# Retention attention in halves of 64 tokens with a state in the middle, and weight decoding inside the raw weight tile

## The chip, the cores and the metric

The kernel runs on one core of a Trainium2 chip. The metric is the device time of one execution in microseconds (us), median of several runs. The core has five engines that run side by side and wait for each other on semaphores: TensorE (PE in the profile; PEld is its loading of weights), VectorE (DVE), ScalarE (ACT), GpSimd (POOL) and SyncE (SP), which issues the DMAs here.

## The reference

A retention (linear attention with decay) over 4 sequences of 768 tokens with 8 heads of 64, and behind it a feed-forward layer on all 3072 tokens whose activation is a ratio of two polynomials:

```python
for t in range(S):                                   # S = 768, D = 64, 8 heads, 4 sequences
    state = gamma * state + einsum('bhd,bhe->bhde', k[:, :, t], v[:, :, t])
    y[:, :, t] = scale * einsum('bhd,bhde->bhe', q[:, :, t], state)
x = y.transpose(0, 2, 1, 3).reshape(3072, 512)
h = x @ w_in                                         # 512 -> 2048
g = (a0 + a1*h + a2*h*h + a3*h**3) / (1 + abs(b0)*abs(h) + abs(b1)*h*h + 1e-6)
out = g @ w_out                                      # 2048 -> 512
```

## The kernel before, in words

**Chunks and slots.** The attention is done in 24 chunks of 128 tokens, six to a sequence (`C = 6`, the chunk's place in its sequence is `c`). Four chunks make a block of 512 tokens, six blocks in all. The feed-forward layer runs in 96 slots: a slot `(n, f)` takes block `n` and 128 of the 2048 inner units. A slot has `gemm_in` (12 matmuls 128x512 into a PSUM tile `ph`, of which there are two), the polynomials on ACT, DVE and POOL (`poly_scalar`, `poly_vector`, `ratio_scalar`, `ratio_vector`, `split`), and `gemm_out` (12 matmuls into four `po` tiles), which runs three slots later (`LAG = 3`). Full precision comes from splitting each operand into a high and a low part (`xh`/`xl`, `gh`/`gl`, two parts of each weight), hence 12 matmuls where four would do.

**Order.** All five queues are in the order in which the code is written. `opening()` does the four chunks of block 0 and decodes the first weight tiles; then `run()` goes over the slots. The chunks of block `n` lie in the slots ahead of it, in two parts each: part 0 (scores and mask) behind a slot's `gemm_out`, part 1 (the rest) between a later slot's `gemm_in` and `gemm_out`. Blocks 1 and 2 have a part in every slot (slots 0 to 7 and 24 to 31), blocks 3 to 5 in every second slot from 32 to 78. Slots 8 to 23 and 80 to 95 hold no attention.

**One chunk.** `scores` (L249) multiplies keys and queries, in quarters of the PE array (64 rows by 64 columns, `64*64` in the profile): late keys with late queries, and early keys with all queries, so half of its matmuls have 128 columns to stream and half have 64. The two other results go to the banks `pa`. `mask` (L266) multiplies them on DVE with a causal table into `aT`. `recall` (L290) multiplies the state from before the chunk with all 128 queries, in quarters of 128 columns. `outer` (L276) forms keys times values over all 128 tokens, in halves of the array (`128*64`). `values` (L320) multiplies `aT` with the values: the later half over 128 rows (`128*64`), the earlier over 64 (`64*64`). Quarters that write into one bank at once are kept apart by a semaphore that SP passes on (`gate`, L315). `update` (L338) adds the new outer product to the single tile `state`; `scale_state` on POOL lets it decay. `x_out` splits the result into `xh` (ACT) and `xl` (DVE). Each of these f32 matmuls is two records in the profile, two passes over the same columns: 8 matmuls are `x16` there.

**Weights.** A weight tile arrives as 64-bit floats, two 32-bit words `raw[:, :, 0]` (low) and `raw[:, :, 1]` (high), one DMA of 512 KB, 32 tiles in all. ACT reads some bits of the low word into `t` (`decode_low`, L132) and the high word into `u` (`decode_high`, L140). DVE joins them in two instructions (`decode_join`, L148 and L151, called the two joins below). ACT rounds to the high part (`decode_split`, L164), POOL takes the difference (`decode_rest`, L171). A tile is decoded in each of the slots 3 to 24. `u` lies in PSUM:

```python
    def u_bank():
        if not opened:                       # in opening(): the two ph banks
            return early_bank("u", f"ph{count['u'] % 2}", U32)
        ...
        return bank("u", U32)                # later: the two banks that pa and px use in turn
```

`bank` (L61) hands the two banks `bank0` and `bank1` out in turn, to `pa`, to `px` and to `u`; whoever comes next waits until the last owner is done.

**Loads.** Each chunk needs `kT`, `qT`, `v` and `k`, 256 KB each, double-buffered. In the opening SP issues them in this order, chunk by chunk, with weight tiles between; in `run()` `kT` of chunk `i + 2` comes in part 0 of chunk `i`, the other three in part 1. POOL scales `qT` and `v` (L227, L233).

Of the kernel before, what the change touches and what calls it, by code (L numbers as in the profile page):

```python
# [16 lines left out]
P = 128  # L17
# [4 lines left out]
def tile_retention_rational_ffn(  # L22
# [35 lines left out]
    count = {"ph": 0, "bank": 0, "u": 0}  # L58
    opened = []

    def bank(name, dtype=F32):  # L61
        tag = "ph" if name == "ph" else "bank"
        count[tag] += 1
        return ps.tile([P, TB], dtype, name=name, tag=f"{tag}{count[tag] % 2}")
# [5 lines left out]
    def u_bank():  # L70

        if not opened:
            count["u"] += 1
            return early_bank("u", f"ph{count['u'] % 2}", U32)
        if len(opened) < 2:
            count["u"] += 1
            return early_bank("u", f"po{count['u'] % 2}", U32)
        if len(opened) < 3:
            return early_bank("u", f"po{SPB - 1}", U32)
        return bank("u", U32)  # L80

    def px_banks(i):
        if len(opened) < 2:
            return [early_bank("px", f"po{r + 2 * (i % 2 or i >= SPB)}") for r in range(2)]
        return [bank("px") for _ in range(2)]


    causal_sb = const.tile([P, 3, HP], F32, name="causal_sb")
# [7 lines left out]
    state = const.tile([P, NP, D], F32, name="state")  # L96
# [37 lines left out]
    def decode_high(i):  # L134
        if i >= len(tiles):
            return


        us[i] = u_bank()
        nc.scalar.activation(  # L140
            us[i].bitcast(F32), raws[i][:, :, 1].bitcast(F32), AF.Abs, scale=2.0 ** -112
        )
# [58 lines left out]
    def load_k_t(i):  # L201
        load_part(i, "kT", kT, 0, [P, NP, P])

    def load_rest(i):
        load_part(i, "qT", qT, 1, [P, NP, P])
        load_part(i, "v", v, 3, [P, H, D])
        if i % C < C - 1:
            load_part(i, "k", kk, 2, [P, H, D])
# [10 lines left out]

    def quarters(r, j):  # L220
        odd = (r + j) % 2
        lo, hi = slice(odd * HP, (odd + 1) * HP), slice((1 - odd) * HP, (2 - odd) * HP)
        return lo, hi, slice(0, 2 + odd, 1 + odd), 1 + odd
# [12 lines left out]

    def scale_state(i):
        if i < NSTEP and i % C > 0:
            nc.gpsimd.tensor_mul(
                state, state, sdec_sb.unsqueeze(2).broadcast_to([P, NP, D])  # L240
            )

    def pa_banks(i):
        st = steps[i]
        if "banks" not in st:
            st["banks"] = [bank("pa") for _ in range(2)]
        return st["banks"]

    def scores(i):  # L249
        st = steps[i]  # L250
        pa = [x[:, : 3 * P].rearrange("p (a b t) -> p a b t", a=2, b=3) for x in pa_banks(i)]
        for late in range(2):
            for a in range(2):
                for j in range(2):
                    for r in range(2):
                        rows = slice(r * D, (r + 1) * D)
                        lo, hi, both, own = quarters(r, j)
                        nc.tensor.matmul(  # L258
                            pa[r][hi, a, own] if late else pa[r][lo, a, both],
                            st["kT"][rows, 2 * a + j, late * HP : (late + 1) * HP],  # L260
                            st["qT"][rows, 2 * a + j, late * HP :],
                            start=True, stop=True,
                        )
        st["pa"] = pa

    def mask(i):  # L266
        st = steps[i]
        for r in range(2):
            st["aT", r] = at.tile([P, 2, 3, HP], F32, name="aT")
            nc.vector.tensor_mul(  # L270
                st["aT", r], st["pa"][r],
                causal_sb.unsqueeze(1).broadcast_to([P, 2, 3, HP]),
            )


    def outer(i, first):  # L276
        st = steps[i]
        if first or i % C == 0:
            st["px"] = px_banks(i)
        if i % C < C - 1:  # L280
            pk = st["pk"] = st["px"][1][:, TB // 2 :].rearrange("p (h d) -> p h d", d=D)
            for aj in range(NP):
                for r in range(2):
                    h = 4 * (aj // 2) + 2 * r + aj % 2
                    nc.tensor.matmul(  # L285
                        pk[r * D : (r + 1) * D, aj], st["k"][:, h], st["v"][:, h],
                        start=(first or i % C == 0), stop=True, skip_group_check=True,
                    )

    def recall(i, first):  # L290
        st = steps[i]
        if i % C > 0:
            if first:
                st["px"] = px_banks(i)

            for a in range(2):
                for j in range(2):
                    for r in range(2):
                        rows = slice(r * D, (r + 1) * D)
                        st["recalled"] = nc.tensor.matmul(  # L300
                            st["px"][r][j * D : (j + 1) * D, a * P : (a + 1) * P],
                            state[rows, 2 * a + j], st["qT"][rows, 2 * a + j],
                            start=(a == 0), stop=False, skip_group_check=True,
                        )
# [10 lines left out]
    def gate(i):  # L315
        if i % C > 0:
            steps[i]["gate"] = nc.sync.nop()
            after(steps[i]["gate"], steps[i]["recalled"])

    def values(i, lates=(1, 0)):  # L320
        st, c = steps[i], i % C
        for late in lates:
            for a in range(2):
                for j in range(2):
                    for r in range(2):
                        lo, _, _, own = quarters(r, j)
                        s, b = (slice(0, P), own) if late else (lo, 0)
                        t = a * P + late * HP
                        x = nc.tensor.matmul(  # L329
                            st["px"][r][j * D : (j + 1) * D, t : t + HP],  # L330
                            st["v"][s, 4 * a + 2 * r + j], st["aT", r][s, a, b],
                            start=(c == 0 and late == 1 and a == 0),
                            stop=(c == 0 or a == 1), skip_group_check=True,
                        )
                        if late == 0 and c > 0 and (a, j, r) == (0, 0, 0):
                            after(x, st["gate"])

    def update(i):  # L338
        if i % C < C - 1:
            if i % C == 0:  # L340
                return nc.vector.tensor_copy(state, steps[i]["pk"])
            return nc.vector.tensor_add(state, steps[i]["pk"], state)

    def x_parts(i, r):
# [20 lines left out]
    def opening():  # L365
# [14 lines left out]
        for i in range(SPB):  # L380
# [4 lines left out]
            if i + 1 < SPB:  # L385
                fill(i + 1, FILL[1])
# [325 lines left out]
```

## Time and profile before

| | us |
|---|---|
| median of three runs (637.66, 639.0, 639.3) | 639.0 |
| the profiled execution: from its first to its last instruction | 636.5 |
| PE busy | 614.6 |
| ACT busy | 440.4 |
| DVE busy | 437.3 |
| POOL busy | 362.7 |

What an execution takes around its instructions isn't in the trace; the median is 2.5 us over the profiled execution's span. A row of a group reads: line, engine, operation, output <- inputs, sizes, count, then busy time of the group and mean duration of one instruction, then how long the engine stood idle ahead of such instructions and who ended that. In the chain of work that ended last, and in the timeline, a row is: start, duration (us), engine, what. Neighbouring matmuls overlap, so distances between starts say more of PE than durations do.

### The profile page before, as it was taken

To read this page: it belongs to the slowest core of one execution; us is meant where nothing else is said; L and a number is where in the kernel's file an instruction comes from. 1 tells how busy PE (TensorE), PEld (TensorE's weight loads), DVE (VectorE), ACT (ScalarE), POOL (GpSimd) and SP (SyncE) were. 2 spreads that over 40 slices of the span, in tenths; PEclk is the share of its full clock that TensorE was granted. 3 is DMA by queue.
4 is the path that set the end of the run, shared out by engine and by line. 5 is a ranking of instruction groups with operands and counts; after the bars stand their busy time and mean duration, and the time that the engine had idled before them with its cause. 6 is when DMAs were issued, how large, how long until landed. Compare 5 with 4: busy or idle time off the path is not lost.

```text
span 636.5 us, 11515 instructions
## 1 busy us (share of the span) xinstructions
PE 614.6 (97%) x4508; PEld 495.8 (78%) x4508; DVE 437.3 (69%) x684; ACT 440.4 (69%) x721; POOL 362.7 (57%) x311
## 2 busy tenths in 40 slices
PE   7598999999999999999999999999999999999997
PEld 4386778888877878788888878888878888888885
DVE  3668888888887666766666676666666656766663
ACT  2678889889886557566657676675766576777773
POOL 3858678888866554563644554544456443444442
PEclk9888999999999999999999999999999999999999
DMA  9976672001016222310110321121301000100001
GB/s 319 399 262 233 220 274 90 1 1 66 1 52 198 67 68 83 132 50 19 50 50 18 117 67 34 35 51 34 112 22 34 2 0 2 57 10 1 1 1 66
DMA packets 24389, 52.48 MB, mean 82 GB/s; under 512 B 3088, under 2 KB 3216, under 8 KB 24336
## 3 DMA queue, kind: packets, MB, share of 16 engines
q1 hardware_dynamic: 24336, 51.76, 23.8%
q8 instruction: 35, 0.57, 0.4%
q14 instruction: 18, 0.15, 0.1%
HBM read 43.36 MB, written 8.39 MB: 81 GB/s over the span
## 4 chain that ended last, share of the span: by engine, by line
PE 70%; ACT 10%; DVE 9%; issue 4%; DMA 1%; POOL 0%; POOLq 0%; SPq 0%; DVEq 0%; ACTq 0%
PE ph L424 32%; PE po L479 30%; PE px L329 3%; ACT ph L453 2%; ACT s L452 2%; DVE q L456 2%; DVE ph L457 2%; ACT t L132 2%; DVE p L458 2%; PE pa L258 2%; PE px L300 1%; PE px L285 1%; DMA v<-in_v 1%; DVE p L447 1%; ACT s L441 1%
## 5 line engine op out<-in xcount | busy, mean ns | idle before, releaser
L442 POOL TENSOR_TENSOR q<-q,s 128x512 f32<-128x512 f32 x96 | 124.6, 1298 | 216.9 <-ACT s L441 209.8
L424 PE MATMUL ph<-xh,w 128*128 128x512 f32 (+2 forms) x776 | 211.4, 395 | 5.2 <-DVE t L151 3.4
L479 PE MATMUL po<-w,gh 128*128 128x512 f32 x768 | 200.2, 393 | 0.0
L424 PEld LDWEIGHTS ph<-xh,w 128*128 128x128 f32 x776 | 145.3, 191 | 36.3 <-ACT u L140 3.6
L479 PEld LDWEIGHTS po<-w,gh 128*128 128x128 f32 x768 | 142.7, 188 | 30.5 <-POOL w L171 0.2
L435 ACT ACTIVATE q<-ph 128x512 f32<-128x512 f32 x96 | 57.2, 596 | 116.1 <-PE ph L424 115.9
L447 DVE TENSOR_TENSOR p<-ph,p 128x512 f32<-128x512 f32 x96 | 66.1, 689 | 95.1 <-ACT p L443 95.0
L464 POOL TENSOR_TENSOR gl<-p,gh 128x512 fp32r<-128x512 f32 x96 | 124.7, 1299 | 7.3 <-issue 4.5
L479 PE MATMUL po<-w,gl 128*128 128x512 f32 x384 | 110.6, 390 | 0.2 <-POOL gl L464 0.2
L424 PE MATMUL ph<-xl,w 128*128 128x512 f32 (+2 forms) x388 | 104.7, 392 | 0.0
L456 DVE SCALAR_TENSOR_TENSOR q<-q,qcon,ph 128x512 f32<-128x512 f32 x96 | 71.4, 743 | 48.4 <-ACT ph L453 48.1
L424 PEld LDWEIGHTS ph<-xl,w 128*128 128x128 f32 x388 | 74.0, 192 | 15.5
L452 ACT ACTIVATE s<-q,qcon 128x512 f32<-128x512 f32 x96 | 69.4, 723 | 22.9 <-POOL q L442 22.9
L479 PEld LDWEIGHTS po<-w,gl 128*128 128x128 f32 x384 | 72.1, 188 | 15.6 <-POOL gl L464 0.6
L448 DVE SCALAR_TENSOR_TENSOR p<-p,par_sb,ph 128x512 f32<-128x512 f32 x96 | 71.8, 748 | 3.4
L443 ACT ACTIVATE p<-ph,par_sb 128x512 f32<-128x512 f32 x96 | 73.3, 764 | 0.0
L457 DVE SCALAR_TENSOR_TENSOR ph<-p,par_sb,ph 128x512 f32<-128x512 f32 x96 | 71.9, 749 | 0.0
L458 DVE SCALAR_TENSOR_TENSOR p<-q,ph 128x512 f32<-128x512 f32 x96 | 65.9, 686 | 3.3
L463 ACT CAST gh<-p 128x512 fp32r<-128x512 f32 x96 | 58.7, 612 | 13.5 <-DVE p L458 13.5
L441 ACT ACTIVATE s<-q,babs 128x512 f32<-128x512 f32 x80 | 65.4, 817 | 2.7
L453 ACT ACTIVATE ph<-s 128x512 f32<-128x512 f32 x96 | 57.8, 602 | 11.5 <-DVE p L448 2.2
L171 POOL TENSOR_TENSOR w<-t,w 128x512 fp32r<-128x512 f32 x32 | 41.3, 1294 | 0.8 <-ACT w L164 0.8
(38 smaller groups left out, 426.6 us busy)
## 6 DMA issues: line engine op xcount, KB each, us to landing
raw<-in_w_in SPq DMA_DIRECT2D x16, 512.0 KB, 5.5
raw<-in_w_out SPq DMA_DIRECT2D x16, 512.0 KB, 6.8
kT<-in_kT SPq DMA_DIRECT2D x24, 256.0 KB, 2.8
qT<-in_qT SPq DMA_DIRECT2D x24, 256.0 KB, 3.2
v<-in_v SPq DMA_DIRECT2D x24, 256.0 KB, 3.2
out<-o SPq DMA_DIRECT2D x24, 256.0 KB, 2.3
k<-in_k SPq DMA_DIRECT2D x20, 256.0 KB, 3.5
half<-o SPq DMA_DIRECT2D x8, 256.0 KB, 2.2
```

The costliest lines, as they stand in the source:

```text
L424: nc.tensor.matmul(ph[:, t0:t1], w1[f][:, part, kt * P : (kt + 1) * P], x[:, kt, t0:t1], start=(i == 0), stop=(i == 3 * NP - 1),)
L441: nc.scalar.activation(s, q, AF.Identity, bias=babs[:, 0:1], scale=babs[:, 1:2])
L442: nc.gpsimd.tensor_mul(q, q, s)
L443: nc.scalar.activation(p, ph, AF.Identity, bias=par_sb[:, 2:3], scale=par_sb[:, 3:4])
L447: nc.vector.tensor_mul(p, ph, p)
L448: nc.vector.scalar_tensor_tensor(p, p, par_sb[:, 1:2], ph, ALU.add, ALU.mult)
L452: nc.scalar.activation(s, q, AF.Abs_reciprocal_sqrt, bias=qcon[:, 0:1])
L456: nc.vector.scalar_tensor_tensor(q, q, qcon[:, 0:1], ph, ALU.add, ALU.mult)
L457: nc.vector.scalar_tensor_tensor(ph, p, par_sb[:, 0:1], ph, ALU.add, ALU.mult)
L458: nc.vector.scalar_tensor_tensor(p, q, 2.0, ph, ALU.subtract, ALU.mult, reverse0=True)
L464: nc.gpsimd.tensor_sub(gl, p, gh.bitcast(F32))
L479: nc.tensor.matmul(o_tiles[n][tt], g_[:, tt * P : (tt + 1) * P], w2[f][:, part], start=(first and m == 0), stop=(last and m == 2),)
```

## The change

**Attention in halves.** A chunk is cut into two halves of 64 tokens. `scores` now multiplies only keys and queries of the same half: 16 matmuls of 64 columns in quarters. What an earlier half sends to a later one goes through a state: `outer` (now over 64 tokens per matmul, in quarters, 16 matmuls) makes an outer product for each half, and `carry` adds them on DVE to two states, `middle` (before the second half) and `begin` (before the next chunk). `recall` takes each half's queries with the state ahead of that half, 16 matmuls of 64 columns; half of them run in part 0 ("crossed": row half `r` of the array writes the bank `1 - r`), half in part 1, so that in each part a row half always writes the same bank. `values` is 16 matmuls of 64 columns in quarters. The gate through SP is gone.

**A chunk ahead.** `outer` of chunk `i + 1` now runs in part 1 of chunk `i`, and so do `carry(i + 1)`, the scaling of `begin` for chunk `i + 2` and, as before, of `v` for `i + 2`. In the last chunk of a sequence `outer` runs for the first half alone, which loads 128 KB of `k` where nothing was loaded before.

**Banks.** A chunk has one pair of banks for everything (`pair`): scores, and later the next chunk's outer products, in the first half of each bank, the result in the second. In `run()` this is always `bank0` and `bank1`; in the opening the `po` banks.

**Decode scratch.** `u` is now the raw tile's own low words, in SBUF.

**Loads.** The order in a chunk is `v`, `k`, `kT`, `qT`, all in part 1.

The core of the diff:

```diff
-    def u_bank():
-...
-    def px_banks(i):
-...
+    def pair(i):
+        tags = [f"po{r + 2 * (i % 2)}" if 0 <= i < SPB else f"bank{r}" for r in range(2)]
+        if i not in pairs:
+            pairs[i] = [early_bank("pair", t) for t in tags]
+        return pairs[i]
...
-        us[i] = u_bank()
+        us[i] = raws[i][:, :, 0]
...
-            load_part(i, "k", kk, 2, [P, H, D])
+            rows = P if i % C < C - 1 else HP
+            nc.sync.dma_start(out=st["k"][:rows], in_=kk[i // C, i % C][:rows])
...
+    def outer(i):
+        pk = [x[:, : TB // 2].rearrange("p (h d) -> p h d", d=D) for x in pair(i - 1)]
+        for aj in range(NP):
+            for th in range(2 if i % C < C - 1 else 1):
+                for r in range(2):
+                    h = head(aj // 2, r, aj % 2)
+                    nc.tensor.matmul(
+                        pk[th][half(r), aj], st["k"][half(th), h], st["v"][half(th), h],
+                        start=(aj == 0), stop=True, skip_group_check=True,
+                    )
+    def carry(i):
+        st["from", 1] = at.tile([P, NP, D], F32, name="middle", bufs=1)
+        if c == 0:
+            nc.vector.tensor_copy(st["from", 1], st["pk"][0])
+        else:
+            nc.vector.tensor_add(st["from", 1], st["pk"][0], st["from", 0])
+        if c < C - 1:
+            state = at.tile([P, NP, D], F32, name="begin")
+            steps.setdefault(i + 1, {})["from", 0] = state
+            nc.vector.tensor_add(state, st["pk"][1], st["from", 1])
+    def recall(i, crossed):
+        for a in range(2):
+            for j in range(2):
+                for r in range(2):
+                    kh = 1 - r if crossed else r
+                    if ("from", kh) in st:
+                        st["recalled"] = nc.tensor.matmul(
+                            px(i, kh)[half(j), a, r],
+                            st["from", kh][half(r), 2 * a + j],
+                            st["qT"][half(r), 2 * a + j, half(kh)],
+                            start=opens(i, kh, j), stop=False, skip_group_check=True,
+                        )
     def scores(i):
+        for n in range(NP):
+            for kh in range(2):
+                for r in range(2):
+                    nc.tensor.matmul(
+                        pa[r][half(kh), n], st["kT"][half(r), n, half(kh)],
+                        st["qT"][half(r), n, half(kh)],
+                        start=opens(i, 1 - r, kh), stop=True, skip_group_check=True,
+                    )
...
         for i in range(SPB):
-            outer(i, True)
-            recall(i, False)
-            values(i, (1,))
-            steps[i]["gate"] = update(i)
-            values(i, (0,))
-            scale_state(i + 1)
+            values(i)
+            recall(i, False)
+            outer(i + 1)
+            carry(i + 1)
+            scale_v(i + 2)
+            scale_state(i + 2)
             for j in OPENING[i - 1] if i else ():
                 decode_rest(j)
             if i + 2 <= SPB:
                 scale_q(i + 2)
-            scale_v(i + 2)
...
             if part == 1:
-                recall(chunk, True)
-                outer(chunk, False)
-                gate(chunk)
                 values(chunk)
+                recall(chunk, False)
+                outer(chunk + 1)
...
             if part == 0 and k >= LAG:
+                recall(chunk, True)
                 scores(chunk)
-                load_k_t(chunk + 2)
...
             if part == 1:
-                update(chunk)
+                carry(chunk + 1)
                 x_out(chunk)
-                load_rest(chunk + 2)
+                load_by_token(chunk + 2)
+                load_by_dim(chunk + 2)
                 scale_q(chunk + 1)
-                scale_state(chunk + 1)
+                scale_state(chunk + 2)
                 scale_v(chunk + 2)
```

How the order of the instructions moves is shown at three places. The first is PE in part 1 of chunk 12, the first of the third sequence, between a slot's `gemm_in` (L424) and `gemm_out` (L479). Before:

```order
L424 MATMUL ph<-xh,w 128x512 x4
L285 MATMUL px<-v,k 64x64 x8
L329 MATMUL px<-aT,v 64x64 x16
L479 MATMUL po<-w,gh 128x512 x8
L479 MATMUL po<-w,gl 128x512 x4
```

After, at the same place (`gemm_in` is L418, `gemm_out` L473):

```order
L418 MATMUL ph<-xh,w 128x512 x4
L329 MATMUL pair<-aT,v 64x64 x16
L281 MATMUL pair<-qT,middle 64x64 x4
L252 MATMUL pair<-v,k 64x64 x16
L473 MATMUL po<-w,gh 128x512 x8
L473 MATMUL po<-w,gl 128x512 x4
```

`values` (L329 in both) comes first now, `recall` (L281) behind it, and `outer` (L252, of the next chunk) last, with twice the matmuls; in a chunk with a state from an earlier one `recall` is eight matmuls, from `begin` and `middle` in turn. The second place is POOL in the opening, from the scaling of chunk 2's queries on; `w` is the low part of a weight tile (`decode_rest`). Before:

```order
L227 TENSOR_TENSOR qT<-qT,qdec_sb 128x512
L233 TENSOR_TENSOR v<-v,vdec_sb 128x512
L239 TENSOR_TENSOR state<-state,sdec_sb 128x256
L171 TENSOR_TENSOR w<-t,w 128x512
L227 TENSOR_TENSOR qT<-qT,qdec_sb 128x512
```

After:

```order
L212 TENSOR_TENSOR qT<-qT,qdec_sb 128x512
L218 TENSOR_TENSOR v<-v,vdec_sb 128x512
L230 TENSOR_TENSOR begin<-begin,sdec_sb 128x256
L158 TENSOR_TENSOR w<-t,w 128x512
L212 TENSOR_TENSOR qT<-qT,qdec_sb 128x512
```

The rows read alike, but the last one has moved against the others: the `v` here is chunk 3's where it was chunk 2's, the state that of chunk 3 where it was chunk 2's, and only the queries keep their place, so chunk 3's queries are now scaled behind chunk 3's values. The third place is SP in the opening, the loads of chunk 1. Before:

```order
L199 DMA kT<-in_kT 128x512
L199 DMA qT<-in_qT 128x512
L199 DMA v<-in_v 128x512
L199 DMA k<-in_k 128x512
L114 DMA raw<-in_w_in 128x1024
```

After:

```order
L186 DMA v<-in_v 128x512
L198 DMA k<-in_k 128x512
L186 DMA kT<-in_kT 128x512
L186 DMA qT<-in_qT 128x512
L101 DMA raw<-in_w_in 128x1024
```

The queries are the fourth of a chunk's loads where they were the second.

More of the change, by code (lines that the diff above doesn't have):

```diff
@@ L68, in early_bank @@
         return pool.tile([P, TB], dtype, name=name, tag=tag)
-    def u_bank():
[L72 to L80, printed above, removed]
-    def px_banks(i):
[L83 to L88, printed above, removed]
+    def pair(i):
[3 more added lines that the diff above has]
+        return pairs[i]
+    causal_sb = const.tile([P, HP], F32, name="causal_sb")
     qdec_sb = const.tile([P, NP, P], F32, name="qdec_sb")
@@ L239, in scale_state, with opens @@
             nc.gpsimd.tensor_mul(
-                state, state, sdec_sb.unsqueeze(2).broadcast_to([P, NP, D])
-            )
-    def pa_banks(i):
-        st = steps[i]
-        if "banks" not in st:
-            st["banks"] = [bank("pa") for _ in range(2)]
-        return st["banks"]
+                steps[i]["from", 0], steps[i]["from", 0],
+                sdec_sb.unsqueeze(2).broadcast_to([P, NP, D]),
+            )
+    def opens(i, bank, quarter):
+        seen = touched.setdefault(i, set())
+        new = (bank, quarter) not in seen
+        seen.add((bank, quarter))
+        return new
@@ L249, in scores @@
     def scores(i):
         st = steps[i]
[L251 to L263, printed above, removed]
@@ L264, in scores @@
-        st["pa"] = pa
-    def mask(i):
+        pa = st["pa"] = [
+            pair(i)[1 - r][:, : TB // 2].rearrange("p (n t) -> p n t", t=HP) for r in range(2)
+        ]
+        for n in range(NP):
[6 more added lines that the diff above has]
+                    )
@@ L267, in mask @@
+    def mask(i, ordered=False):
         st = steps[i]
         for r in range(2):
-            st["aT", r] = at.tile([P, 2, 3, HP], F32, name="aT")
-            nc.vector.tensor_mul(
+            st["aT", r] = at.tile([P, NP, HP], F32, name="aT")
+            x = nc.vector.tensor_mul(
                 st["aT", r], st["pa"][r],
-                causal_sb.unsqueeze(1).broadcast_to([P, 2, 3, HP]),
+                causal_sb.unsqueeze(1).broadcast_to([P, NP, HP]),
             )
[L276 to L304, printed above, removed]
+            if ordered and r == 1:
+                after(x, st["recalled"])
```

128 lines of the change are left out of this document (59 added, 69 removed).

## The prediction, as it was written before the changed kernel ran

> **What bounds the kernel now.** I read the page's first part, then the chain of work that ended last, then the groups by shape, then the stages.
>
> ```profile
> span 636.5 us, 11515 instructions
> PE 614.6 (97%) x4508; PEld 495.8 (78%) x4508; DVE 437.3 (69%) x684; ACT 440.4 (69%) x721; POOL 362.7 (57%) x311
> ```
>
> PE is busy almost all the time, so what PE no longer has to do comes off the end, as long as nothing else becomes late. The chain shows what attention costs in a steady stage. Three chunks of the last blocks: one with a state before it and an outer product after it, then the last and the first of a sequence.
>
> ```profile
> 288.64 2.72 PE po L479 x12
> 291.36 0.83 PE pa L258 x32
> 292.19 2.95 PE ph L424 x12
> ...
> 300.57 0.60 PE px L300 x16
> 301.17 0.62 PE px L285 x16
> 301.79 0.91 PE px L329 x32
> 302.69 2.95 PE po L479 x12
> ...
> 376.05 0.60 PE px L300 x16
> 376.65 1.05 PE px L329 x32
> ...
> 400.75 0.61 PE px L285 x16
> 401.36 0.91 PE px L329 x32
> ```
>
> Twelve dense matmuls take 2.72, but 2.95 behind attention. Part 0 thus costs 0.83 + 0.23 = 1.06. Part 1 costs 0.60 + 0.62 + 0.91 + 0.23 = 2.36 in a full chunk, 0.60 + 1.05 + 0.23 = 1.88 in the last of a sequence (no outer), 0.61 + 0.91 + 0.23 = 1.75 in the first (no recall). A full chunk costs 3.42. The sum below is made against this execution's span, 636.5; the median of the runs shown is 639.0, so I add 2.5 at the end.
>
> **Attention on PE.** What a pass costs comes from the groups by shape:
>
> ```profile
> L300 PE MATMUL px<-qT,state 64*64 64x128 f32 x320 | 15.0, 290 | 0.8 <-DVE t L151 0.6 <-DVE aT L270 0.2
> L285 PE MATMUL px<-v,k 128*64 128x64 f32 x320 | 14.0, 231 | 1.6 <-PE ph L424 0.9 <-POOL v L233 0.4
> L329 PE MATMUL px<-aT,v 64*64 64x64 f32 x384 | 11.4, 234 | 3.9 <-DVE state L342 3.9
> ```
>
> Each comes in bursts of 16 passes. Quarters with 64 columns: 24 bursts, 11.4 / 24 = 0.475, less the last pass itself (0.234) leaves 0.24 for 16 passes, so four quarters run abreast and four passes take 0.06. Quarters with 128 columns: 15.0 / 20 - 0.29 = 0.46, four passes 0.115. Halves with 64 columns: 14.0 / 20 - 0.231 = 0.47, two passes 0.06. A full chunk before is 0.46 + 0.24 (scores), 0.46 (recall), 0.47 (outer), 0.47 + 0.24 (values): 2.34. After, all is quarters of 64: 128 passes, 32 fours of 0.06, 1.92, of which part 0 has 0.72 and part 1 1.20. Part 0 before is 0.70 of passes and 0.36 for entering and leaving the shape. Part 1 before changes shape four times, after only twice, so I give each part after 0.36. A full chunk costs 1.92 + 0.72 = 2.64 and saves 0.78. In the first chunk of a sequence recall has half the matmuls, but from one state, so on two quarters of four: no less time. It still costs 2.64, saving 2.81 - 2.64 = 0.17; the last one (outer for one half, two quarters) saves 2.94 - 2.64 = 0.30. The slots hold chunks 4 to 23: 13 full, 3 first, 4 last, 10.1 + 0.5 + 1.2 = 11.8, and 0.48 more since no outer follows the last chunk: 12.3. In slots 0 to 2 PE waits for the polynomials of earlier slots, so chunk 4 and part 0 of chunk 5 give nothing back: **-11.2**.
>
> The Trainium skill ("TensorE: Matmul & The Clock Gate", section "Wait — 56ns, not 53.3ns?") says that matmuls never start closer than about 25 ns apart however few columns they have. By it 128 passes would take at least 3.2 us, an estimate from that page, and a chunk would become dearer instead. This trace disagrees: with four quarters in turn it starts 16 passes in 0.24, 15 ns apart, so the sum goes by the rows.
>
> **Waits for banks.** Joining a weight holds a bank that attention needs next:
>
> ```profile
> PE px L300 <- DVE t L151: 0.6, 2, 0.4
> ...
> PE px L285 <- PE ph L424: 0.9, 1, 0.9
> ```
> ```profile
> 69.50 0.69 DVE L151 SCALAR_TENSOR_TENSOR t<-raw,u 128x512 uint32<-128x512 uint32 x1
> ...
> 70.29 0.69 PE L285 MATMUL px<-v,k 128*64 128x64 f32 x16 [0.93 <-PE ph L424]
> ```
>
> The second wait is put down to PE itself, but it ends when the join ends, at 70.19. With `u` in the raw tile both go: **-1.5**. The new pair is one buffer: scores of the next chunk need `x_out` of this one, which ends over a slot (5.44) earlier, so I see no new wait.
>
> **The opening.**
>
> ```profile
> 20.00:25.00 5.00, 3.68 (x98) 2.65 (x96) 3.33 (x8) 3.62 (x7) 4.09 (x4) 1.00 1.04 396
> 50.70:54.10 3.40, 3.26 (x20) 2.50 (x12) 3.33 (x7) 3.37 (x7) 2.60 (x3) 0.50 0.53 208
> ```
> ```profile
> L233 POOL TENSOR_TENSOR v<-v,vdec_sb 128x512 f32<-128x512 f32 x24 | 25.0, 1043 | 18.7 <-DMA v<-in_v 18.7
> L239 POOL TENSOR_TENSOR state<-state,sdec_sb 128x256 f32<-128x256 f32 x20 | 12.2, 609 | 2.9 <-DVE state L342 1.8 <-DVE state L341 1.1
> ```
> ```profile
> 20.73 1.27 POOL L227 TENSOR_TENSOR qT<-qT,qdec_sb 128x512 f32<-128x512 f32 x1 [1.76 <-DMA qT<-in_qT]
> ...
> 23.01 1.02 DVE L270 TENSOR_TENSOR aT<-pa,causal_sb 128x384 f32<-128x384 f32 x2 [1.64 <-PE pa L258]
> 23.53 1.29 POOL L171 TENSOR_TENSOR w<-t,w 128x512 fp32r<-128x512 f32 x1
> ...
> 29.62 0.76 DVE L356 TENSOR_TENSOR xl<-px,xh 128x256 fp32r<-128x256 f32 x2 [1.88 <-ACT xh L352]
> 31.91 1.62 PE L424 MATMUL ph<-xh,w 128*128 128x384 f32 x4 [3.40 <-DVE t L151]
> ...
> 37.82 0.45 PE L258 MATMUL pa<-qT,kT 64*64 64x128 f32 x8
> ```
>
> DMA is full (396 GB/s, so 256 KB take 0.66), and the first slot ends at 37.8. It started only at 31.91 because its `ph` bank held a `u`; that wait of 3.4 goes. What is late next is chunk 3. Its first load lands about 20.0 (0.66 ahead of the queries at 20.7). That is now `v`; POOL scales it (1.04), then the state (0.61) and a weight's low part (1.29), and only then the queries (1.27): done at 24.2 instead of 22.0. So the mask ends at 26.2, not 24.0. From there to the end of chunk 3's `xl` it was 30.4 - 24.0 = 6.4, and a second add in `carry` (0.42) comes in: 33.0. By then three quarters of the first `gemm_in`, which need chunks 0 to 2 alone, are done, and the last part takes 0.8: 33.8 in place of 37.8. But PE idles from about 30 to 33, and behind such a pause the trace shows a granted clock of 0.50 for one 3.4 us stage (50.7 to 54.1 above): 1 us lost again. **-3.0**, between -5 (no cold stage) and 0 (the stretch from mask to `xl` grows by what the joins lose, below).
>
> **Small ones.**
>
> ```profile
> PE ph L424 <- DVE p L458: 1.5, 3, 0.8
> L342 DVE TENSOR_TENSOR state<-px,state 128x256 f32<-128x256 f32 x16 | 6.7, 417 | 0.3 <-PE px L329 0.3
> L140 ACT ACTIVATE u<-raw 128x512 f32<-128x512 f32 x33 | 20.7, 626 | 0.0
> ```
>
> Of the 1.5, 0.7 (two waits in blocks 3 and 4) hangs on POOL waiting for `v`; as the first of the loads it comes half a microsecond sooner: **-0.7**. DVE: two adds of 0.42 where one was, two masks of 0.42 where two of 0.51 were: +0.24 a chunk, under DVE's idle time (31%) in the attention slots. ACT writes `u` to SBUF rather than PSUM: no row shows it; a little less than 0.63 or up to 0.1 more each, in 16 slots between 0 and +1.5; I take 0.
>
> **The joins.** This term decides. Every DVE instruction that runs beside POOL in this trace reads at most one operand from SBUF, the other from PSUM; the one with two (the scaling of chunk 0's queries) ran before POOL's first arithmetic. Now both joins read two from SBUF, the raw tile and `t`. POOL reads only SBUF. In slots 8 to 23, without attention, they overlap:
>
> ```profile
> 89.63:176.67 87.04, 87.02 (x383) 71.47 (x382) 77.47 (x117) 77.85 (x132) 72.98 (x66) 1.00 0.15 56
> ```
> ```profile
> 117.68 1.29 POOL L464 TENSOR_TENSOR gl<-p,gh 128x512 fp32r<-128x512 f32 x1
> ...
> 117.96 0.69 DVE L148 SCALAR_TENSOR_TENSOR u<-u,t 128x512 uint32<-128x512 uint32 x1
> ...
> 118.69 0.69 DVE L151 SCALAR_TENSOR_TENSOR t<-raw,u 128x512 uint32<-128x512 uint32 x1
> ...
> 118.93 1.29 POOL L171 TENSOR_TENSOR w<-t,w 128x512 fp32r<-128x512 f32 x1
> ...
> 119.90 0.75 DVE L456 SCALAR_TENSOR_TENSOR q<-q,qcon,ph 128x512 f32<-128x512 f32 x1 [0.52 <-ACT ph L453]
> ...
> 122.07 0.62 ACT L463 CAST gh<-p 128x512 fp32r<-128x512 f32 x1 [0.56 <-DVE p L458]
> ```
>
> PE sets the pace, 87.04 / 16 = 5.44 a slot. No row tells whether a DVE read of two SBUF operands and POOL's reads get in each other's way. From below: they don't, 0. From the middle: they take turns, and nothing else is lost. Then POOL's 72.98 and the joins' 16 x 1.38 = 22.1 follow one another: 95.1 for the 16 slots instead of 87.0, **+8.1**. From above: each join stands behind a whole POOL instruction. The first waits for `gl` until 118.97 and ends at 119.66, `w` goes next to 120.95, the second join ends at 121.64, and L456 starts 1.8 later than now. That is not absorbed: L456 waits for ACT and ACT's `gh` for L458 already, each slot, so 16 x 1.8 = 29. I take the middle: ACT (77.85 / 16 = 4.9 a slot) and DVE (4.8) have about half a microsecond of play, and the loop can shift until joins find POOL's pauses. In the opening and slots 0 to 7, 16 tiles more, I add **+1.5**, as POOL's waits for DMA and ACT leave room (0 to +6).
>
> The Trainium skill ("SBUF — State Buffer", section "Who interferes with whom") says that a DVE instruction with two SBUF inputs contends with a GpSimd instruction that reads SBUF, and that whoever comes second is blocked for the whole of the first. By it the sum is the middle or the upper end; no run here shows it yet.
>
> **Sum.** -11.2 - 1.5 - 3.0 - 0.7 + 8.1 + 1.5 = -6.8; 636.5 - 6.8 = 629.7, and 2.5 for what lies around: **632** us.
>
> **Rivals.** *No meeting*: joins and POOL don't touch. The 9.6 go: **622.6**. For it: POOL's durations are even in this trace; against: the trace has no case of it, since no operands were placed so. *Joins behind whole POOL instructions*, slower: the mechanism above, in slots 8 to 23. It decides once a slot's second join ends later than `s` and `ph` on ACT let L456 start, by over 0.4 a slot. 29 for 8.1: 632.2 + 20.9 = **653**. For it: `gl` starts just ahead of the first join and `w` just ahead of the second's end, so the present order is the bad one. *Quarters in long bursts don't stay four abreast*: runs of quarters were 16 to 32 passes, now 48 and 80. At the pace of halves, 0.03 a pass, 128 take 3.84, 1.92 more in 20 chunks: 632 + 38 = **670**. Against: part 0 already runs 32 quarter passes in 0.83.
>
> **How the numbers follow.** Taking turns 0.38, with 625 to 641 of its own; no meeting 0.26 (617 to 627); behind whole instructions 0.33 (642 to 662); short-of-four quarters 0.03. A measurement of this kernel can tell about 0.3%, 1.9 us, from no change. Faster by that: three quarters of the first case and all of the second, 0.54; the same 0.09; slower 0.37. The range leaves out the lowest third of "no meeting" (0.08) and the top of the slow cases (0.12): 620 to 656.
>
> **What would show it.** Right: part 1 about 1.5 and part 0 about 1.06 in the chain; no wait of PE for L138 (the second join); first slot over by 34 to 36. The joins' mean duration (0.69) and the length of slots 8 to 23 (5.44) decide between the cases: 0.69 and 5.44 is "no meeting"; joins or POOL stretched, slots of about 5.9 is the forecast, 7 and more the slow rival. Wrong would be a wait that I have not priced: POOL's scaling of `begin`, on which the next chunk's recall hangs, or ACT, with its 4.9 of 5.44.

## The result, and the profile after

The changed kernel takes 643.7 us (643.1 to 643.8), the kernel before, run on the same chip, 639.2 (637.7 to 639.7): a ratio of 1.0069, 95% interval 1.0051 to 1.0088, so 0.7% slower. The first rows of the page show a longer span, although PE has less to do (614.6 before) and DVE more (437.3 before).

```profile
span 641.9 us, 13020 instructions
PE 608.4 (95%) x5276; PEld 487.8 (76%) x5276; DVE 468.5 (73%) x708; ACT 445.9 (69%) x721; POOL 382.2 (60%) x311
```

Cut by the starts of `gemm_in` in slots 0, 8, 24, 32 and 80, the two profiled executions compare so (us):

| stage | before | after | difference |
|---|---|---|---|
| opening, to slot 0 | 31.9 | 31.8 | -0.1 |
| slots 0 to 7 | 57.7 | 66.3 | +8.6 |
| slots 8 to 23 | 87.6 | 95.7 | +8.1 |
| slots 24 to 31 | 58.3 | 55.6 | -2.7 |
| slots 32 to 79 | 300.9 | 292.9 | -8.1 |
| slots 80 to 95 and the end | 100.1 | 99.7 | -0.4 |

**The late blocks** do what was forecast. The chain of work that ended last, at chunk 13's part 1 and chunk 14's part 0 (start, duration, engine, what):

```profile
289.16 0.62 PE pair L329 x32
289.78 0.23 PE pair L281 x16
290.01 0.47 PE pair L252 x32
290.48 2.95 PE po L473 x12
...
304.31 0.39 PE pair L281 x16
304.70 0.47 PE pair L296 x32
305.17 0.90 PE ph L418 x3
```

With the 0.23 that the next dense matmuls take longer, part 1 costs 1.55 (2.36 before) and part 0 1.09 (1.06 before). Between 249 and 542 us, PE's waits (those of its weight loads apart) are a single row, and it isn't for a join:

```profile
PE ph L418 <- ACT xh L343: 0.7, 1, 0.7
```

**The joins** are stretched, and so is POOL. Groups by shape, mean in ns behind the busy time (before: joins 0.69 each, POOL's `gl` and `w` 1.29 to 1.31 in slots 8 to 23):

```profile
L458 POOL TENSOR_TENSOR gl<-p,gh 128x512 fp32r<-128x512 f32 x96 | 133.5, 1390 | 8.3 <-issue 6.5 <-POOL q L436 1.1 <-ACT gh L457 0.7
L158 POOL TENSOR_TENSOR w<-t,w 128x512 fp32r<-128x512 f32 x32 | 48.7, 1525 | 2.1 <-DMA raw<-in_w_out 2.1
L138 DVE SCALAR_TENSOR_TENSOR t<-raw 128x512 uint32<-128x512 uint32 x32 | 44.1, 1377 | 1.8 <-DVE raw L135 0.5
L135 DVE SCALAR_TENSOR_TENSOR raw<-raw,t 128x512 uint32<-128x512 uint32 x32 | 27.5, 860 | 4.9 <-ACT raw L127 4.9
```

How, the timeline of a plain slot shows (start, duration, engine, line, operation):

```profile
129.71 0.69 DVE L135 SCALAR_TENSOR_TENSOR raw<-raw,t 128x512 uint32<-128x512 uint32 x1
129.72 1.83 POOL L458 TENSOR_TENSOR gl<-p,gh 128x512 fp32r<-128x512 f32 x1
...
130.44 1.67 DVE L138 SCALAR_TENSOR_TENSOR t<-raw 128x512 uint32<-128x512 uint32 x1
...
131.52 1.74 POOL L158 TENSOR_TENSOR w<-t,w 128x512 fp32r<-128x512 f32 x1
...
132.03 0.73 DVE L450 SCALAR_TENSOR_TENSOR q<-q,qcon,ph 128x512 f32<-128x512 f32 x1
```

The first join is first by 0.01 and runs undisturbed; `gl` gets 0.53 longer than its 1.30 before, its wait for that join. The second join can't read until `gl` is nearly done (131.55) and ends 0.56 later, at 132.11: a wait of 1.67 - 0.69 = 0.98. `w` comes next and is 0.44 longer. They take turns by almost whole instructions: the later one gets going 0.13 to 0.15 before the earlier one ends. A waiting instruction counts as busy in these records, so the wait shows as a longer duration.

**The first slots** got slower by as much. Busy time in slots 0 to 2, before and after (the stretch, its length, then PE, PEld, DVE, ACT and POOL with their counts, PE's granted clock, the share of DMA and GB/s):

```profile
31.91:51.07 19.16, 15.85 (x176) 13.53 (x176) 12.89 (x22) 14.92 (x26) 11.63 (x11) 0.86 0.71 260
```
```profile
31.84:56.63 24.79, 15.52 (x210) 12.63 (x208) 20.07 (x30) 19.43 (x33) 16.51 (x13) 0.84 0.74 279
```

PE is busy for about as long as before and idles 9.3 instead of 3.3, 6.5 of it in waits for DVE. The two longest, in PE's timeline (releaser in brackets):

```profile
44.74 0.69 PE L329 MATMUL pair<-aT,v 64*64 64x64 f32 x32 [2.88 <-DVE aT L306]
...
49.13 1.19 PE L418 MATMUL ph<-xh,w 128*128 128x512 f32 x2 [3.00 <-DVE p L452]
```

### The profile page after: what moved, and what is told of

It reads as the page before. It is cut to its first block, busy times and chain, and to the rows that moved or that the text cites. A ratio compares the mean times of both kernels' runs of the same rounds, so it can differ in the third digit from the quotient of the medians.

```text
span 641.9 us, 13020 instructions
## 1 busy us (share of the span) xinstructions
PE 608.4 (95%) x5276; PEld 487.8 (76%) x5276; DVE 468.5 (73%) x708; ACT 445.9 (69%) x721; POOL 382.2 (60%) x311
## 4 chain that ended last, share of the span: by engine, by line
PE 66%; DVE 22%; ACT 5%; issue 3%; POOL 1%; DMA 1%; SPq 0%; POOLq 0%; DVEq 0%; ACTq 0%
PE ph L418 31%; PE po L473 30%; DVE t L138 5%; DVE raw L135 3%; DVE p L442 2%; DVE p L441 2%; DVE q L450 2%; DVE ph L451 2%; DVE p L452 2%; PE pair L281 2%; PE pair L329 2%; PE pair L252 1%; PE pair L296 1%; ACT ph L447 1%; DVE xl L347 1%
## 5 line engine op out<-in xcount | busy, mean ns | idle before, releaser
L436 POOL TENSOR_TENSOR q<-q,s 128x512 f32<-128x512 f32 x96 | 125.9, 1311 | 207.9 <-ACT s L435 206.5
L418 PE MATMUL ph<-xh,w 128*128 128x512 f32 (+2 forms) x776 | 214.4, 399 | 11.7 <-ACT xh L343 6.1
L473 PE MATMUL po<-w,gh 128*128 128x512 f32 x768 | 201.2, 393 | 1.5 <-POOL w L158 1.5
L418 PEld LDWEIGHTS ph<-xh,w 128*128 128x128 f32 x776 | 144.6, 191 | 48.0 <-DVE p L452 7.9
L473 PEld LDWEIGHTS po<-w,gh 128*128 128x128 f32 x768 | 142.5, 188 | 33.2 <-POOL w L158 3.2
L458 POOL TENSOR_TENSOR gl<-p,gh 128x512 fp32r<-128x512 f32 x96 | 133.5, 1390 | 8.3 <-issue 6.5
L473 PE MATMUL po<-w,gl 128*128 128x512 f32 x384 | 110.6, 390 | 0.2 <-POOL gl L458 0.2
L418 PE MATMUL ph<-xl,w 128*128 128x512 f32 (+2 forms) x388 | 105.7, 395 | 0.0
L418 PEld LDWEIGHTS ph<-xl,w 128*128 128x128 f32 x388 | 74.3, 192 | 16.1
L473 PEld LDWEIGHTS po<-w,gl 128*128 128x128 f32 x384 | 72.1, 188 | 15.7 <-POOL gl L458 0.6
L457 ACT CAST gh<-p 128x512 fp32r<-128x512 f32 x96 | 58.8, 613 | 11.2 <-DVE p L452 11.1
L447 ACT ACTIVATE ph<-s 128x512 f32<-128x512 f32 x96 | 57.8, 602 | 11.5 <-DVE p L442 2.5
L158 POOL TENSOR_TENSOR w<-t,w 128x512 fp32r<-128x512 f32 x32 | 48.7, 1525 | 2.1 <-DMA raw<-in_w_out 2.1
```

Of the source, the lines that this page charges most:

```text
L418: nc.tensor.matmul(ph[:, t0:t1], w1[f][:, part, kt * P : (kt + 1) * P], x[:, kt, t0:t1], start=(i == 0), stop=(i == 3 * NP - 1),)
L436: nc.gpsimd.tensor_mul(q, q, s)
L458: nc.gpsimd.tensor_sub(gl, p, gh.bitcast(F32))
L473: nc.tensor.matmul(o_tiles[n][tt], g_[:, tt * P : (tt + 1) * P], w2[f][:, part], start=(first and m == 0), stop=(last and m == 2),)
```

## The experiments

"A" is the theory that joins with both operands in SBUF and POOL's instructions shut each other out. Ratios are to the kernel before, with 95% intervals.

**`u` in the raw tile, and nothing else.** The kernel before with

```diff
-        us[i] = u_bank()
+        us[i] = raws[i][:, :, 0]
```

> The kernel before with one edit: `u` is the raw tile's low words (SBUF) instead of a PSUM bank; attention, loads and order stay as before. Theory A (a join with both operands in SBUF and a POOL instruction shut each other out, instruction by instruction): in slots 8 to 23 the second join takes about 1.67 and the POOL instruction behind it 1.75 to 1.82, as in the changed kernel, and these 16 slots take 95 to 96 instead of 87.6; the opening loses the 3.4 that PE waited for the bank but gets stretched joins, -3 to +4; together 641 to 650 against 639. Rival B (the changed kernel's long slots come from its new attention or its new order, not from the place of `u`): slots 8 to 23 stay at 5.44, all joins at 0.69, and without the waits for banks the kernel takes 634 to 637.

Measured: 652.2, ratio 1.0227 (1.0209 to 1.0244). Groups by shape:

```profile
L151 DVE SCALAR_TENSOR_TENSOR t<-raw 128x512 uint32<-128x512 uint32 x32 | 44.5, 1390 | 1.4
L148 DVE SCALAR_TENSOR_TENSOR raw<-raw,t 128x512 uint32<-128x512 uint32 x32 | 27.2, 851 | 4.1 <-ACT raw L140 4.1
```

The same stretched joins without any of the new attention, and slots 12 to 18 at 5.73. Slots 8 to 23 take 94.8 (+7.3), slots 0 to 7 64.3 (+6.6). B falls. A's mechanism is seen, but its range (641 to 650) was too low: it allowed the opening and the first slots +4 at most, and they cost 1.4 + 6.6 = 8.0, since slot 0 starts at 33.3, not earlier, in spite of the freed bank. So the one line costs 652.2 - 638.4 = 13.8, and the rest of the change is worth 652.2 - 643.7 = 8.5 (9.3 when each is set against the runs of the kernel before that were made beside it).

**`u` back in PSUM, late and early.** The changed kernel with one of

```diff
-        us[i] = raws[i][:, :, 0]
+        if 15 <= i < 31:
+            us[i] = early_bank("u", f"bank{i % 2}", U32)
+        else:
+            us[i] = raws[i][:, :, 0]
```
```diff
-        us[i] = raws[i][:, :, 0]
+        if i < 10:
+            us[i] = early_bank("u", "bank0" if i < 4 else f"po{i % 2}", U32)
+        else:
+            us[i] = raws[i][:, :, 0]
```

> The changed kernel with `u` in the two PSUM banks of the pairs, for the weight tiles that are decoded in slots 8 to 23 alone, where no attention needs them. Theory A: joins there are back at 0.69, POOL's instructions at 1.29 to 1.31, the slots at 5.44: 8 less in slots 8 to 23, nothing else moves, 635 to 637. Rival B: the slots stay at about 5.74 and the time at 643 to 644.

> The changed kernel with `u` in PSUM for the ten tiles that are decoded in the opening and in slots 0 to 2 (bank0 for the first four, po0 and po1 for the others). Theory A: the loss in the opening is joins that wait for POOL and hold up DVE's queue, so a pair of joins takes 1.4 instead of 3.0, the loop of joins, rounding on ACT and the next chunk's xl is shorter by about 1 to 1.5 in each of its turns, and slot 2 starts at 43 to 46 instead of 49.1: 637 to 640. Rival B (the opening is late because of the order of the loads, chunk 1's queries land 2 us later): slot 2 starts at 48 or later, 642 to 644.

Measured, late: 636.5, ratio 0.9975 (0.9966 to 0.9985). Slots 8 to 23 take 89.2 instead of 95.7. Both kinds of join stand in one trace, by shape:

```profile
L141 DVE SCALAR_TENSOR_TENSOR t<-raw 128x512 uint32<-128x512 uint32 x16 | 17.5, 1097 | 1.2 <-DVE raw L138 0.5
L138 DVE SCALAR_TENSOR_TENSOR raw<-raw,t 128x512 uint32<-128x512 uint32 x16 | 16.3, 1020 | 5.1 <-ACT raw L130 5.1
L138 DVE SCALAR_TENSOR_TENSOR u<-u,t 128x512 uint32<-128x512 uint32 x16 | 11.1, 691 | 0.0
L141 DVE SCALAR_TENSOR_TENSOR t<-raw,u 128x512 uint32<-128x512 uint32 x16 | 11.0, 687 | 0.5
```

The last row still reads `raw` from SBUF and writes `t` to SBUF; only `u` is elsewhere, and it isn't stretched. What is left above 87.6 is slot 8 (7.19 for 5.49 before). PE had waited 3.57 for an `xh` just ahead of it, and the row of slot 8 has a granted clock of 0.76, where slots 8 to 23 of the kernel before have 1.00:

```profile
97.61:104.80 7.19, 7.19 (x25) 5.75 (x25) 5.47 (x9) 5.04 (x9) 4.81 (x6) 0.76 0.68 272
```

0.24 of 7.19 is 1.7. So 6.4 of the 8.1 are joins of these slots, and 1.7 is PE's slow start after a pause that comes from ahead.

Early: 638.3, ratio 1.0002 (0.9988 to 1.0015). Slot 2 starts at 46.4 instead of 49.1 (43 to 46 was expected), slot 8 at 93.4 instead of 98.2. The two runs also take away what ACT needs longer to write `u` into SBUF (0.68 a tile for 0.63 in PSUM, 1.8 in all); they don't separate that from the joins, but it is small, and ACT is busy for only 82.0 of the 95.7 of slots 8 to 23.

**The order of the loads.** The changed kernel, in the opening with

```diff
-                load_by_token(i)
-                load_by_dim(i)
+                load_by_dim(i)
+                load_by_token(i)
```

and POOL's scalings in the order `q`, `v`, state as before.

> The changed kernel with the opening's order of loads and of POOL's scalings as before (keys and queries first, and the queries scaled before values and state). Theory A: the first chunks come about 2 us sooner, but the joins stay stretched, so 0 to 3 are gained: 641 to 644. Rival B: the opening is back where it was, slot 2 starts at 43 to 46, 636 to 639.

Measured: 641.9, ratio 1.0068 (1.0046 to 1.0090), the same ratio as that of the changed kernel. In its one trace slot 2 starts 3 sooner (46.2), as B had it, and the span is 2.7 shorter; the ratio doesn't confirm a gain, and the time lies in A's range, not in B's. The order isn't the main cause.

**Both, everywhere, and with the old order.** The fifth run joins the second and third. The sixth puts `u` of the tiles of slots 3 to 7 and 24 into `pair(chunk)`, two halves of 256 words; the seventh adds the fourth's order. The core:

```diff
+        elif i < 15 or i == 31 and 8 in pairs:
+            chunk = 8 if i == 31 else (i + 1) // 2
+            us[i] = [x.bitcast(U32)[:, : TB // 2] for x in pair(chunk)]
```

> The changed kernel with `u` in PSUM for the tiles of the opening and slots 0 to 2 (as in the third run) and for those of slots 8 to 23 (as in the second); slots 3 to 7 and 24 keep it in the raw tile. Theory A (each stretched pair of joins costs at its own place): the two gains add, 643.7 - 7.2 - 5.4 = 631, 630 to 633. Rival C (an early gain is lost again in slots 8 to 23, or the late one was possible only because the opening was late): 634 to 637.

> `u` never in the raw tile: beside the fifth run's places, the tiles of slots 3 to 7 and 24 put it into the first halves of the two banks of the chunk that is in work, which lie idle between the mask and the next outer product; each of their joins becomes two of 256 columns. Theory A: slot 7 (11.9 in the changed kernel, 8.6 before), which waits for the joins of slots 6 and 7 through DVE's and ACT's queues, falls to 8 to 9.5, slot 8 to 5.4 to 6, and another 3 to 5 go: 626 to 629. Rival C: slot 7 is long because of the new attention (carry, two halves of x), and stays at 11 or more: 630 to 633.

> The sixth run's kernel with the opening's loads and POOL's scalings in the order of before as well. If the order costs beside the joins (theory A): chunk 1's queries come 2 us sooner and the first slots with them, 1 to 3 less than the sixth run, 624 to 627. If DVE's joins had been the only brake (rival): within 1 of the sixth run.

Measured: 631.2, ratio 0.9886 (0.9856 to 0.9917): the gains add. Then 629.9, ratio 0.9866 (0.9841 to 0.9891), less than the 3 to 5 expected: slot 7 falls to 8.7 and slot 8 to 5.6 as A has it, but slot 4 rises to 7.7 and slots 9 and 10 to 6.5 and 5.9. Then 629.0, ratio 0.9856 (0.9830 to 0.9881), within 1 of the sixth: what the order costs can't be told from nothing. This is the fastest kernel of the study and beats both. Slot 8 starts at 89.6 and 89.5 in these two, where the kernel before has 89.6. Without the line, the rest of the change is worth 638.5 - 629.9 = 8.6, as in the first run.

**`u` in SBUF, side by side.** The changed kernel with

```diff
-        us[i] = raws[i][:, :, 0]
+        us[i] = ff.tile([P, DM], U32, name="u", tag="o", bufs=BUFS["o"])
```

> The changed kernel with `u` in an SBUF tile of its own, 512 words side by side, instead of every second word of the raw tile. Theory A (two operands in SBUF, wherever they lie): the second join still takes about 1.67 beside POOL, slots 12 to 22 stay at 5.74, 642 to 645. Rival D (the stride of two words, or two instructions on one raw tile, makes the joins slow): joins at 0.69 to 0.9, slots at 5.44, 632 to 637.

Measured: 647.7, ratio 1.0147 (1.0121 to 1.0173), joins by shape:

```profile
L138 DVE SCALAR_TENSOR_TENSOR t<-raw,u 128x512 uint32<-128x512 uint32 x32 | 43.0, 1345 | 1.7 <-DVE u L135 0.5
L135 DVE SCALAR_TENSOR_TENSOR u<-u,t 128x512 uint32<-128x512 uint32 x32 | 28.2, 880 | 4.4 <-ACT u L127 4.4
```

The stride isn't it (D falls). It is slower than expected by some 3 at places that A doesn't speak of: the tile shares its buffers with the output tiles, and ACT waits for them to be stored (slots 19 and 20 take 8.3 and 7.2):

```profile
L127 ACT ACTIVATE u<-raw 128x512 f32<-128x512 f32 x33 | 21.9, 664 | 3.5 <-DMA half<-o 3.5
```

**PE's unexplained pauses.** In the opening of the changed kernel, PE's timeline has two pauses inside `values` without a named releaser:

```profile
21.23 0.46 PE L329 MATMUL pair<-aT,v 64*64 64x64 f32 x14 [0.32 <-DVE aT L306]
23.39 0.50 PE L329 MATMUL pair<-aT,v 64*64 64x64 f32 x17 [1.71 <-issue]
...
27.26 0.44 PE L329 MATMUL pair<-aT,v 64*64 64x64 f32 x10 [0.32 <-DVE aT L306]
29.72 0.81 PE L329 MATMUL pair<-aT,v 64*64 64x64 f32 x20 [2.02 <-issue]
```

Two runs put small matmuls on zeros at PE's start, 40 and 8:

```diff
+        bank1 = early_bank("fill", "bank1")
+        z = zeros.bitcast(F32)
+        for n in range(40):
+            r, c = slice(64), slice(64 * (n % 2), 64 * (n % 2) + 64)
+            nc.tensor.matmul(
+                bank1[c, :64], z[r, :64], z[r, :64], start=True, stop=True, skip_group_check=True
+            )
```

> The changed kernel with 40 small matmuls on zeros (80 records on PE, one quarter, no use of the result) added at PE's start, where PE waits for the first loads. It is about PE's two pauses in the opening, 1.71 after 14 of the 32 records of the values of chunk 2 and 2.02 after 10 of those of chunk 3, for which the profile names no releaser. Theory F (PE waits for its own instructions: a 16 KB packet run of the instruction queue lies next to each pause, and a chunk of the opening has about as many instructions as one such block): both pauses move 80 records back in the program, into the outer products of chunk 2 (after about 16 of its 32 records) and of chunk 3 (after about 12), and the values run through; time 641 to 645. Rival G (a wait for data, or for the joins, that the profile didn't name): the pauses stay where they are in the values.

> The same with 8 small matmuls, 16 records. Theory F: the pauses move 16 records back, to the fill or the recall ahead of the values of chunks 2 and 3, where PE waits 0.3 for the mask anyway, so up to that is gained in each: 642 to 644. Rival G: no pause moves, 643 to 644.

Measured with 40: 645.7 (two runs only), ratio 1.0119 (1.0098 to 1.0139). PE's timeline around chunks 2 and 3:

```profile
17.21 0.74 PE L252 MATMUL pair<-v,k 64*64 64x64 f32 x17
20.05 0.60 PE L252 MATMUL pair<-v,k 64*64 64x64 f32 x12 [2.11 <-issue]
...
22.94 1.14 PE L329 MATMUL pair<-aT,v 64*64 64x64 f32 x32 [0.36 <-DVE aT L306]
24.27 0.65 PE L252 MATMUL pair<-v,k 64*64 64x64 f32 x13
26.17 0.80 PE L252 MATMUL pair<-v,k 64*64 64x64 f32 x18 [1.25 <-issue]
```

Both pauses stand in the outer products now, after 17 and 13 records, and the values run through: a place in the program, not in the data. Two more such pauses appear, of 0.99 at 13.0 and of 2.67 at 33.0. Counted in matmul records from PE's first one, they stand behind 222, 348, 473 and 599; in the changed kernel the two stand behind 348 and 474. The instruction queue has one packet of 16 KB between 17.7 and 18.9, beside the pause that ends at 20.05, none from 19 to 23.5, and the next one between 23.5 and 25, beside the pause that ends at 26.17. The first:

```profile
q8 instruction: 1, 0.02, 5.1%
```

With 8: 644.5, ratio 1.0099 (1.0083 to 1.0114). No long pause without a releaser is left: the place behind record 348 is now the start of the values of chunk 2, where PE waits 0.36 for DVE anyway, as F had it. But PE now waits for POOL's queries instead:

```profile
19.12 1.13 PE L296 MATMUL pair<-qT,kT 64*64 64x64 f32 x32 [2.01 <-POOL qT L212]
...
25.62 0.93 PE L296 MATMUL pair<-qT,kT 64*64 64x64 f32 x32 [2.09 <-POOL qT L212]
```

Nothing was gained: slot 0 starts at 30.2 instead of 31.8, but slot 8 at 97.9 instead of 98.2. The places bear F out and G falls, but both times lie above F's ranges (641 to 645 and 642 to 644). The pauses don't set the time here.

**Slots 3 and 4 with `u` in the raw tile.** The seventh run's kernel with the condition above split at tile 12:

```diff
+        elif i < 12:
+            us[i] = [raws[i][:, :, 0]]
```

> The seventh run's kernel (u in PSUM, loads in the old order), but with `u` in the raw tile again for the two tiles of slots 3 and 4, where splitting the joins had made slot 4 longer (7.7 for 6.5 in the fifth run). If slot 4's 1.2 is a loss of its own: 627 to 628.5. If it only moves to slots 7 to 10, which wait for the same queues: 628.5 to 630.

Measured: 630.2, ratio 0.9872 (0.9855 to 0.9888). Slot 4 falls to 6.5, slot 6 rises from 6.4 to 8.1: the time only moved, and the run is a little above its second range (628.5 to 630).

**More work for PE in the first slots.** The seventh run's kernel with

```diff
+            if k < LAG:
+                idle = early_bank("idle", "po3")
+                for _ in range(4):
+                    nc.tensor.matmul(idle, zeros[:, :P], zeros, start=True, stop=True)
```

> The seventh run's kernel with 4 more matmuls of 512 columns on zeros (about 0.43 each) at the end of PE's work in each of the slots 0, 1 and 2, into a bank that is unused there: 5.1 more work for PE. In that kernel no join is stretched, yet slot 8 starts at 89.5 as in the kernel before, though PE has some 6 less to do ahead of it. Theory H (in the first slots the loop of DVE and ACT sets the pace, PE has idle time, so what PE saves or loses there doesn't count): 629 to 630.5. Rival (PE's own work counts there): 633 to 634.

Measured: 630.0 (629.3 to 631.8), ratio 0.9874 (0.9853 to 0.9895), against 0.9856 without. The added matmuls ran closer together than expected, four in about 1.0 (one record is missing here), so some 3 in all and not 5.1:

```profile
37.09 1.04 PE L578 MATMUL idle<-zeros 128*128 128x512 bf16 x3
```

The busy times of slots 0 to 2, without and with them:

```profile
30.36:50.95 20.59, 14.69 (x214) 11.88 (x209) 16.25 (x30) 18.37 (x33) 15.24 (x13) 0.92 0.93 351
```
```profile
31.90:52.26 20.36, 16.62 (x219) 12.88 (x221) 17.09 (x30) 18.68 (x33) 13.59 (x13) 0.92 0.86 330
```

The slots aren't longer, and slot 8 starts at 89.3. ACT is busy for 18.4 of 20.6 there, PE for 14.7. H holds by the trace; the time alone is a weaker witness, because with 3 of added work instead of 5.1 the rival would give about 632, and the intervals of the two ratios overlap.

## Why the prediction went wrong

**Attention on PE: right where PE is the bound.** A full chunk was forecast at 2.64 and costs 1.09 + 1.55 = 2.64. Slots 24 to 79, with chunks 8 to 23, are shorter by 10.8, with the small waits for `v` among it. The prediction set its rows against the floor of about 25 ns between matmuls in the Trainium skill's "TensorE: Matmul & The Clock Gate", section "Wait — 56ns, not 53.3ns?". The new bursts stay below it too: the 80 records of part 1, in quarters of the array, take 0.62 + 0.23 + 0.47 = 1.32, 16.5 ns each, without the 0.23 behind them. (The 11.2 itself is 0.3 short of its own terms: 12.3 less 0.78 for chunk 4, with nothing for part 0 of chunk 5, is 11.5.)

**Joins in slots 8 to 23: the size right by luck, the picture half right.** The +8.1 came, but 6.4 of it is joins and 1.7 is slot 8's slow start. Taking turns was right in that both engines lose. But the play in the loop didn't move the joins into POOL's pauses: in the plain slot shown, each of the three later instructions waits for almost the whole of the earlier one. The Trainium skill ("SBUF — State Buffer", section "Who interferes with whom") says that a DVE instruction with two SBUF inputs contends with a GpSimd instruction that reads SBUF, for ports that are an exclusive lock. The trace agrees but for the last 0.13 to 0.15 of each turn. The slow rival had the mechanism but charged two waits of joins in each slot, 1.8. There is one, of 0.98: the other join starts first and POOL waits. What it costs follows from DVE: 78.0 busy in the 16 slots before is 4.87 a slot, with 0.98 it is 5.85, over PE's 5.44, so DVE takes over the pace. It is busy for 92.6 of the 95.7. The plain slots take 5.74, less than the forecast's 5.9; the rest is in a few longer ones (6.9 in slot 19, 6.7 in slot 23).

**Opening and slots 0 to 7: the step that failed.** The prediction has "In the opening and slots 0 to 7, 16 tiles more, I add **+1.5**, as POOL's waits for DMA and ACT leave room (0 to +6)", and gains of 3.0 for the opening, 1.2 of the 1.5 for banks, and the attention of chunks 5 to 7 (0.9 of the 11.2). It came out at slot 8 starting 8.5 later instead of 3.6 earlier. Two things were wrong.

First, the joins' price. With `u` in PSUM everywhere slot 8 starts at 89.6, with `u` in the raw tile at 98.2: 8.6, not 1.5. In the kernel before, the one line alone moves it from 89.6 to 97.6: 8.0. Both are net of what the freed banks gave. In the opening a pair of joins grows from 1.4 to 3.0, as DVE's timeline shows ahead of chunk 3's mask:

```profile
22.56 1.30 DVE L135 SCALAR_TENSOR_TENSOR raw<-raw,t 128x512 uint32<-128x512 uint32 x1
23.90 1.65 DVE L138 SCALAR_TENSOR_TENSOR t<-raw 128x512 uint32<-128x512 uint32 x1
...
26.45 0.76 DVE L306 TENSOR_TENSOR aT<-pair,causal_sb 128x256 f32<-128x256 f32 x2
...
36.14 0.76 DVE L347 TENSOR_TENSOR xl<-pair,xh 128x256 fp32r<-128x256 f32 x2 [1.48 <-ACT xh L343]
```

Behind the joins in DVE's queue stand `carry`, the mask and `xl`, and behind the rounding on ACT the next `xh`, so each pair delays the next. The mask of chunk 3 ends at 27.2 where 26.2 was forecast, its `xl` at 36.9 where 33.0 was. POOL's waits for DMA gave no room: beside these two joins POOL runs `decode_rest` (22.05 to 23.32) and the scaling of `qT` (23.27 to 24.99).

Second, the gains. Even with no join stretched, slot 8 starts where it did before (89.6). That run has waits for banks again, since `u` lies in them (ACT waits 1.9 for one in the opening, until a join ends). But with the joins stretched in both kernels, and the banks free in both, the rest of the change gains nothing ahead of slot 8 either: 98.2 against the 97.6 of the first experiment. I had read what a chunk costs at 288 us, where PE sets the pace, and counted it in the first slots too. There the chain of before runs over ACT and DVE, from 38 to 51 without any piece of PE; its end:

```profile
46.44 0.76 DVE p L448
...
47.28 0.60 ACT ph L453
...
48.98 0.65 DVE q L456
...
50.33 0.70 DVE p L458
...
51.07 4.42 PE ph L424 x12
```

A bank that comes free earlier, or a shorter burst on PE, adds to PE's idle time there. The run with more work for PE shows it from the other side. So too in the opening: the wait of 3.4 for a bank went, but PE came out of chunk 4's outer products only at 31.8, because chunk 3 was late. The joins, the new order and PE's own pauses all lie ahead of that; how much each did there isn't separated (slot 0 starts at 31.3 with no join stretched, and at 30.4 with the old order as well).

**Sum.** Forecast -6.8 on the span, measured +5.4. Ahead of slot 8 it was -3.6 against +8.5, a difference of 12.1; slots 8 to 23 agree (+8.1), and behind them it was -11.3 against -11.2. The tests named, the joins' duration and the length of slots 8 to 23, pointed to the cause. The wait of PE for the second join is gone, as the forecast had it, without a gain to show for it. For the slots ahead I had named only the end of the first slot's `gemm_in`: 34 to 36 was forecast, it ends at 38.0, where it ended before at 37.8.

What stays open: why splitting the joins lengthens slots 4, 9 and 10 in the sixth run; what the order of the loads alone is worth (nothing by the ratio, 2.7 by the one trace); and what the freed banks would give with no join stretched, since each run that put `u` back into PSUM took banks for it.

## What to carry to other kernels

Moving a scratch operand from PSUM to SBUF wasn't neutral here: where it becomes the second SBUF operand of a VectorE instruction beside a busy GpSimd, add to VectorE's busy time per stage a wait of up to one GpSimd instruction (here 0.98 of 1.30), and compare the sum with the engine that sets the pace. Read a gain from the stage in which it falls: what was saved on PE here counted only where the trace showed it busy throughout. Where scratch must move, look for a PSUM region that is idle for part of the stage; here that turned 0.7% slower into 1.3% faster, and 1.4% with the old order of loads.

## What the runs showed of the hardware that was not expected

The exclusion doesn't depend on the stride of `u` in these runs: with 512 words at a stride of two (the second join 1.38 in the mean) or side by side (1.35) it is the same. One operand in PSUM ends it (0.69), though the instruction still reads one operand from SBUF and writes SBUF. The size of the operands wasn't varied with both in SBUF.

PE paused in dense bursts of small matmuls, for 1.0 to 2.7 us in the run with 40 small matmuls, at places that are fixed in the program and lie 125 or 126 matmul records apart, with as many weight loads 250 to 252 instructions. The Trainium skill ("Runtime: NRT & Kernel Launch", section "Instruction fetch mechanics") says that instructions come in blocks of 16 KB, 256 of them, and that crossing into the next is mostly hidden. The packets of 16 KB beside the pauses and the distance between them agree with the blocks, nearly; "hidden" doesn't hold in these bursts. That the packets are PE's isn't shown: the profile has one instruction queue without the name of an engine.
